# An RWKV-6 attention feeding a GELU MLP: third token blocks paired from the first tile on

## Chip, cores and metric

The kernel runs on one core of one Trainium2 chip. The metric is the device time of one execution in microseconds (us). Before the change it is 604.43 us (median of three runs, 604.32 to 604.50). The profile is one execution with a span of 601.6 us from the first to the last instruction; the granted TensorE clock was full throughout.

Short names in what follows: PE is TensorE, DVE is VectorE, ACT is ScalarE, SP is SyncE.

## What is computed

A recurrent attention over 768 time steps (batch 4, 8 heads, head size 48), and then a two-layer MLP with exact GELU on its output, 3072 tokens of width 384, hidden width 2048:

```python
for t in range(S):                                   # attention, per batch and head
    cur = einsum('bhd,bhe->bhde', u[None] * k[t], v[t])
    y[t] = einsum('bhd,bhde->bhe', r[t], state + cur)
    state = w[t][..., None] * state + einsum('bhd,bhe->bhde', k[t], v[t])

x = y.transpose(0, 2, 1, 3).reshape(3072, 384)       # bridge
h = x @ w_in                                         # 3072x384 @ 384x2048
g = 0.5 * h * (1 + erf(h / sqrt(2)))
out = g @ w_out                                      # 3072x2048 @ 2048x384
```

All values are float32.

## The kernel before

The tokens are worked in eight tiles of 384 (x = 0 to 7). `attention(x)` makes one tile's attention output `xT`; `mlp(x)` turns it into 384 rows of the result. Both are generators: each `yield` ends a step, and a driver decides which step of the one is issued between which steps of the other. While the MLP of tile x-1 runs, the attention of tile x is woven into it. [...]

In the second product of the MLP, a tile has three blocks of 128 tokens. Blocks 0 and 1 are multiplied with `w_out` as a 2x2 block matrix product with seven instead of eight block products (Winograd's form, with sums made beforehand by DVE). The third block of a tile cannot be paired within its tile, so it is paired with the third block of the next tile, which gives one more product of that kind. The tile that comes first of a pair (`waits`) computes two of the products and keeps its GELU output in `alone`; the second (`ends`) computes the other five. Before, the pairs are tiles (1,2), (3,4), (5,6). The first tile (x = 0) multiplies all its three blocks in the plain way, the last (x = 7) its third block.

```python
NX = 8; T = 384; NF = 16; HF = 8; HM = 192; BANK = 512
ps = ...  # PSUM, tag "mm": two banks, shared by h_ps, o_ps and the y_ps of one part
pd = ...  # PSUM, tag "d": three pairs of banks, for the attention

def mlp(x):
    halves = x > 0
    waits, ends = x % 2 == 1 and x < NX - 1, x % 2 == 0 and x > 0
    final = x == NX - 1
    if final:
        h_halves()        # first product of the last tile, itself with seven of eight products
    for group in (() if final else (0, 2, 1, 3) if halves else range(4)):     # 16 steps
        for f in range(group * FG, (group + 1) * FG):
            # h_ps = w_in block f times xT: three matmuls of 384 columns
            t = T - 128 if waits else T
            nc.scalar.activation(out=gs[group][:, f % FG, 0:t], in_=h_ps[:, 0:t], func=AF.Gelu)
            if waits:
                nc.scalar.activation(out=alone[:, f], in_=h_ps[:, t:], func=AF.Gelu)
            yield
    if final:             # the third block of the last tile, alone: 16 matmuls of 384 columns
        ... nc.tensor.matmul(o_ps, lhsT=block(2, f // HF, f % HF), rhs=w_out_sb[:, f, :], ...)
        nc.scalar.copy(out=o_sb, in_=o_ps); store(x * T + 256, o_sb)
        yield
    if halves:            # seven products of 8 matmuls of 192 columns, a step each (steps 16 to 22)
        ...
    if waits:             # two products, steps 23 and 24
        _, o2, o1 = psum(), psum(), psum()
        product(o2, of_alone(0), of_w(0, 0), True); nc.scalar.copy(out=p1_alone, in_=o2)
        yield
        product(o1, of_alone(1), of_w(1, 0), True)
        nc.vector.tensor_add(o_sb[:, 0:HM], o1, p1_alone); store(...)
        yield
    elif ends:            # five products, steps 23 to 27
        ...
    elif not final:       # x = 0: blocks 0 and 1 together (steps 16 to 31), then block 2 (32 to 47)
        for blocks in (0, 1), (2,):
            o_ps = [ps.tile([128, BANK], F32, name="o_ps", tag="mm", bufs=2)[:, 0:DM] for _ in blocks]
            for f in range(NF):
                for i, o in zip(blocks, o_ps):
                    nc.tensor.matmul(o, lhsT=block(i, f // HF, f % HF), rhs=w_out_sb[:, f, :], ...)
                if f < NF - 1:
                    yield
            for i, o in zip(blocks, o_ps):
                o_sb = wk.tile([128, DM], F32, name="o_sb", bufs=2)
                nc.vector.tensor_copy(out=o_sb, in_=o); store(x * T + i * 128, o_sb)
            yield
```

The last stretch of `attention(x)` issues the products with the states (PE, into `y_ps`) and takes the result out of PSUM. From tile 1 on it does the latter on ACT, with DMAs that carry a part of it to other partitions:

```python
        nc.tensor.matmul(ys[b][0][c % 2]..., lhsT=src[...], rhs=rc[...], ...)    # 48 of them
        ...
        copy = nc.vector.tensor_copy if x == 0 else nc.scalar.copy
        copy(out=xT[s, pair, :]..., in_=y[s])               # six copies of 48x384 (x > 0)
        ...
        nc.scalar.copy(out=ysb..., in_=y)                   # one of 128x384, before the six
        (nc.scalar if z * NJ + j > (2 if x == 0 else 3) else nc.sync).dma_start(out=xT[...], in_=ysb[...])
```

Tiles 0 and 1 do the lower triangle of the attention in six levels (h = 1 to 32), each with products on PE, an update of r and k by decays on DVE (one instruction), and a copy into `a_sb`. Later tiles do two levels of four. In tile 0, which works its heads in two units, the k of the last level is then transposed on PE, and r is used much later, for the products with the states.

The driver (cut), and the sums of blocks of `w_out`, which DVE makes once, in eight instructions a step each:

```python
def w_sums():        # sums[0] to sums[3]: eight tensor_sub of 128x768, one to a step
    ...
    shares = chain(weight_in(gate=True), second, weight_in(gate=True), weight_in(gate=True))
    ...
    convert()
    for unit in (0, 0, 1, 0, 0, 1, 1, 0, 1):
        next(units[unit])
    keep_warm(6, True)
    convert()

    for x in range(1, NX):
        place = [1, 3, 5, 7, 9, 11, 13, 15, 18, 20, 26, 32] if x == 1 else [1, 6, 8, 13, 15, 16, 18, 18, 20, 21]
        place_next = [38, 47] if x == 1 else [21, 24] if x % 2 == 0 else [25, 27]
        loads = load(x + 1, nc.scalar if x > 1 else nc.sync)
        times = range(20, 30) if x == 1 else (2, 3, 4, 5, 16, 17, 18, 19, 20, 21)
        more = iter(())
        for step, _ in enumerate(mlp(x - 1)):
            if x == 1 and step == 2 * NF - 2:
                make_quarter_masks(); more = w_sums()
            next(more, None)
            if x == 1 and step in (0, 2, 4, ..., 24):
                convert()                        # a piece of the weights, four DVE and two ACT instructions
            if step in times:
                next(loads, None)                # a piece of tile x+1
            while place and place[0] <= step:
                place.pop(0); next(slots, None)  # a step of attention(x)
            while place_next and place_next[0] <= step:
                place_next.pop(0); next(following, None)     # the first two steps of attention(x+1)
```

Of the kernel before, what the change touches and what calls it, by code (L numbers as in the profile page):

```python
# [23 lines left out]
T = 384  # L24
# [20 lines left out]
def kernel(  # L45
# [79 lines left out]
    def load_second(dma):  # L125

        loaded[1] = [None, None]
        for i in range(SHARES):
            s = slice(i * 3 * ALL // SHARES, (i + 1) * 3 * ALL // SHARES)
            nc.vector.memset(bufs[1][:, s.start:s.start + 1], 0.0)  # L130
            dma.dma_start(out=bufs[1][:, s], in_=rkw[1, :, s])
            yield
        load_v(1, dma)
        yield
# [185 lines left out]
    def attention(x, unit):  # L320
# [102 lines left out]
        def halves():  # L423

            for h in LEVELS:
# [14 lines left out]
                t2 = tot[h].rearrange("p (n two) -> p n two", two=2)[:, :, 0:1].to_broadcast(r2.shape)  # L440
                rk = bass.AP(tensor=r2.tensor, offset=r2.offset, ap=[r2.ap[0], [n_u - h, 2]] + list(r2.ap[1:]))
                tt = bass.AP(tensor=t2.tensor, offset=t2.offset, ap=[t2.ap[0], [1, 2]] + list(t2.ap[1:]))
                nc.vector.tensor_mul(rk, rk, tt)  # L443
# [118 lines left out]

        yield from halves() if x < 2 else quarters()
# [89 lines left out]
        if x == 0:  # L653

            inside()
            yield
            chain_states()
            yield
            fences()
        else:  # L660
            chain_states()
            yield
            inside()
            fences()
            yield
# [68 lines left out]
    def h_sums():  # L734
# [14 lines left out]
        for i in range(4):  # L749
            for k in range(2):  # L750
                if i == 0:
                    nc.vector.tensor_add(s(1, k), w(1, 0, k), w(1, 1, k))
                elif i == 1:
                    nc.vector.tensor_sub(s(2, k), s(1, k), w(0, 0, k))
                elif i == 2:
                    nc.vector.tensor_sub(s(3, k), w(0, 0, k), w(1, 0, k))
                else:
                    nc.vector.tensor_sub(s(4, k), w(0, 1, k), s(2, k))
            if i < 3:
                yield  # L760
# [9 lines left out]
    def mlp(x):  # L770
# [5 lines left out]
        waits, ends = x % 2 == 1 and x < NX - 1, x % 2 == 0 and x > 0  # L776
# [24 lines left out]
        def h_halves():  # L801
# [9 lines left out]
            for f in range(HF):  # L811
# [11 lines left out]
                def s(i):  # L823
                    return in_s[i - 1][:, f // FI, f % FI * 128:(f % FI + 1) * 128]
# [12 lines left out]
                for z in late:  # L837
                    gelu(*z)
                multiply(b_6, (s(2), in_t[1]))
# [7 lines left out]
                multiply(b_4, (w(1, 1), in_t[3]), (w(1, 2), last[0]))  # L847
                nc.vector.tensor_add(c21, b_4, u3)
                gelu(1, 0, c21)
                multiply(b_0, (w(1, 2), last[1]))  # L850
                nc.vector.tensor_add(c22, b_0, u5)
                gelu(1, 1, c22)
# [60 lines left out]
        if final:  # L913
            o_ps = ps.tile([128, BANK], F32, name="o_ps", tag="mm", bufs=2)[:, 0:DM]
            order = [f for f in range(NF) if f % HF < HF - 1] + [HF - 1, NF - 1]
            for n, f in enumerate(order):
                nc.tensor.matmul(o_ps, lhsT=block(2, f // HF, f % HF), rhs=w_out_sb[:, f, :], start=(n == 0), stop=(n == NF - 1))  # L917
            o_sb = wk.tile([128, DM], F32, name="o_sb", bufs=2)
            nc.scalar.copy(out=o_sb, in_=o_ps)
            store(x * T + 256, o_sb)  # L920
            yield


        if halves:
            row0 = x * T
# [41 lines left out]


        if waits:
            _, o2, o1 = psum(), psum(), psum()  # L970
# [34 lines left out]
        elif not final:  # L1005

            for blocks in (0, 1), (2,):
                o_ps = [ps.tile([128, BANK], F32, name="o_ps", tag="mm", bufs=2)[:, 0:DM] for _ in blocks]
                for f in range(NF):
                    for i, o in zip(blocks, o_ps):  # L1010
                        nc.tensor.matmul(o, lhsT=block(i, f // HF, f % HF), rhs=w_out_sb[:, f, :],  # L1011
                                         start=(f == 0), stop=(f == NF - 1))
                    if f < NF - 1:
                        yield
                for i, o in zip(blocks, o_ps):
                    o_sb = wk.tile([128, DM], F32, name="o_sb", bufs=2)
                    nc.vector.tensor_copy(out=o_sb, in_=o)  # L1017
                    store(x * T + i * 128, o_sb)
                yield
# [5 lines left out]
    shares = chain(weight_in(gate=True), second, weight_in(gate=True), weight_in(gate=True))  # L1025
# [19 lines left out]
    convert()  # L1045

    for unit in (0, 0, 1, 0, 0, 1, 1, 0, 1):
        next(units[unit])
# [6 lines left out]

    for x in range(1, NX):

        place = [1, 3, 5, 7, 9, 11, 13, 15, 18, 20, 26, 32] if x == 1 else [1, 6, 8, 13, 15, 16, 18, 18, 20, 21]
        place_next = [38, 47] if x == 1 else [21, 24] if x % 2 == 0 else [25, 27]
        loads = load(x + 1, nc.scalar if x > 1 else nc.sync)  # L1060

        times = range(20, 30) if x == 1 else (2, 3, 4, 5, 16, 17, 18, 19, 20, 21)
        following = attention(x + 1, 0) if x + 1 < NX else iter(())
        more = iter(())
        for step, _ in enumerate(mlp(x - 1)):
# [4 lines left out]
            next(more, None)  # L1070
# [10 lines left out]
            if x == NX - 1:  # L1081

                if step == 18:
                    more_h = h_sums()
                for _ in range({18: 1, 22: 2, 25: 1}.get(step, 0)):
                    next(more_h)
# [65 lines left out]
```

## Time and profile before

| What | Before |
|---|---|
| time, median of three | 604.43 us |
| span of the profile | 601.6 us |
| PE busy, matmuls | 586.7 us (98%) |
| PE weight loads busy | 455.5 us (76%) |
| DVE busy | 468.4 us (78%) |
| ACT busy | 178.9 us (30%) |
| moved by DMA | 46.72 MB, 78 GB/s in the mean |

The busy row of an engine is its share of the whole span; whether an engine bounds a stage is read from the stage. One matmul of float32 shows as two instructions in the profile, so the counts of matmuls there are twice those of the code. The stages that matter, in us from the start: tile 0's attention up to 42.9, `mlp(0)` from 42.9 to 125.3, then `mlp(1)` to `mlp(6)` with 65 or 73 us each, and `mlp(7)` from 541.1 to the end.

### The profile page before, as it was taken

The page shows a single profiled execution, that of the slowest core. Times are in us where ns is not written, and L with a number is a line of the kernel's source. Part 1 is how long each engine was busy: PE and PEld are TensorE (multiplying, and loading weights), DVE is VectorE, ACT ScalarE, POOL GpSimd, SP SyncE. Part 2 cuts the span into 40 slices and gives each one's busy share as a digit, 9 for nine tenths or more (in the row PEclk, how much of TensorE's full clock was granted, in tenths as well). Part 3 has the DMA queues.
Part 4 walks back from the last instruction along what each step waited for, and adds up shares of the span by engine and source line. Part 5 has one row for each costly group of instructions (what it writes and reads, how often), then busy time and mean ns, then how long its engine had stood idle before and what let it go on. Part 6 is the DMA issues. An engine that isn't in the chain of part 4 may idle for free.

```text
span 601.6 us, 16117 instructions
## 1 busy us (share of the span) xinstructions
PE 586.7 (98%) x6993; PEld 455.5 (76%) x7008; DVE 468.4 (78%) x896; ACT 178.9 (30%) x414; POOL 8.4 (1%) x24
## 2 busy tenths in 40 slices
PE   8779999999999999999999999999999999999997
PEld 4556566656798669986699568995689668999977
DVE  8979999998866978488884987679786888665701
ACT  2446476213223322213222232113222133024400
POOL 3100000000000000000000000000000000000000
PEclk9999999999999999999999999999999999999999
DMA  5775348111141305203052304213052002010000
GB/s 201 253 239 194 110 162 297 38 46 60 25 123 45 92 2 111 73 21 93 1 112 73 99 1 83 87 36 92 3 111 73 8 1 40 16 38 8 1 14 26
DMA packets 50566, 46.72 MB, mean 78 GB/s; under 512 B 31680, under 2 KB 35904, under 8 KB 50496
## 3 DMA queue, kind: packets, MB, share of 16 engines
q1 hardware_dynamic: 33152, 29.31, 15.8%
q10 hardware_dynamic: 17344, 16.39, 10.1%
q8 instruction: 55, 0.90, 0.6%
q14 instruction: 15, 0.12, 0.1%
HBM read 36.24 MB, written 4.72 MB: 68 GB/s over the span
## 4 chain that ended last, share of the span: by engine, by line
PE 71%; DMA 1%; issue 0%; DVE 0%; ACTq 0%
PE o_ps L888 30%; PE h_ps L874 26%; PE b L828 5%; PE d L521 4%; PE o_ps L917 2%; PE kv_ps L598 2%; PE y_ps L639 2%; PE y_ps L677 1%; DMA rkw<-kx 1%; PE d L514 1%; DVE o_sb L960 0%; ACTq L468 0%
## 5 line engine op out<-in xcount | busy, mean ns | idle before, releaser
L874 PE MATMUL h_ps<-xT,w_in_sb 128*128 128x384 f32 x672 | 223.0, 489 | 0.0
L874 PEld LDWEIGHTS h_ps<-xT,w_in_sb 128*128 128x128 f32 x672 | 125.9, 190 | 84.6 <-ACT xT L684 0.4
L877 ACT ACTIVATE g<-h_ps 128x384 f32<-128x384 f32 (+1 forms) x112 | 49.4, 443 | 168.3 <-PE h_ps L874 168.3
L888 PE MATMUL o_ps<-t,s 128*128 128x192 f32 x480 | 81.9, 329 | 0.0
L888 PEld LDWEIGHTS o_ps<-t,s 128*128 128x128 f32 x480 | 77.8, 190 | 0.7
L552 DVE COPY_PREDICATED a_sb<-quarter,d 128x384 f32<-128x384 uint8 (+2 forms) x108 | 45.1, 438 | 2.5
L888 PE MATMUL o_ps<-w_out_sb,g 128*128 128x192 f32 x224 | 38.7, 326 | 0.0
L888 PEld LDWEIGHTS o_ps<-w_out_sb,g 128*128 128x128 f32 x224 | 37.0, 190 | 1.9
L613 DVE SCALAR_TENSOR_TENSOR st<-st,tot_sb,kv_ps 128x48 f32<-128x48 f32 x160 | 29.0, 259 | 4.1 <-PE kv_ps L598 4.1
L1011 PE MATMUL o_ps<-w_out_sb,g 128*128 128x384 f32 x96 | 32.2, 491 | 0.0
L888 PE MATMUL o_ps<-w_out_sb,s 128*128 128x192 f32 x160 | 28.3, 330 | 0.0
L888 PE MATMUL o_ps<-t,g 128*128 128x192 f32 x160 | 27.6, 326 | 0.0
L408 PEld LDWEIGHTS d<-rkw 64*64 64x64 f32 x1152 | 18.6, 134 | 11.8 <-DVE rkw L443 7.8
L1011 PEld LDWEIGHTS o_ps<-w_out_sb,g 128*128 128x128 f32 x96 | 17.8, 190 | 12.3 <-DVE o_sb L1017 0.6
L345 DVE TRANSPOSE_TENSOR_REDUCE rkw<-kx 128x48 f32<-128x1536 f32 (+3 forms) x24 | 26.8, 1155 | 0.2
L521 PEld LDWEIGHTS d<-kx,rkw 64*64 64x64 f32 x1152 | 24.3, 133 | 3.4 <-DVE a_sb L559 1.6
L521 PE MATMUL d<-kx,rkw 64*64 64x96 f32 x1152 | 26.5, 245 | 0.0
L888 PEld LDWEIGHTS o_ps<-t,g 128*128 128x128 f32 x160 | 26.3, 190 | 0.0
L888 PEld LDWEIGHTS o_ps<-w_out_sb,s 128*128 128x128 f32 x160 | 25.9, 190 | 0.4
L408 PE MATMUL d<-rkw 64*64 64x64 f32 (+1 forms) x1152 | 20.9, 221 | 4.6 <-DVE rkw L443 2.9
L534 DVE TENSOR_TENSOR rkw<-rkw,tot_sb 128x768 f32<-128x768 f32 x12 | 11.5, 958 | 17.4 <-PE d L521 17.4
L381 DVE TENSOR_TENSOR rkw<-rkw 128x384 f32<-128x384 f32 (+2 forms) x24 | 23.6, 1004 | 0.4
(148 smaller groups left out, 741.8 us busy)
## 6 DMA issues: line engine op xcount, KB each, us to landing
rkw<-in_rkw_dram ACTq DMA_DIRECT2D x45, 256.0 KB, 2.8
raw<-in_w_out_dram SPq DMA_DIRECT2D x8, 768.0 KB, 4.4
out_dram<-o_sb SPq DMA_DIRECT2D x21, 192.0 KB, 1.9
raw<-in_w_in_dram SPq DMA_DIRECT2D x5, 768.0 KB, 6.0
v_in<-in_v_dram ACTq DMA_DIRECT2D x5, 584.0 KB, 3.7
raw<-in_w_in_dram SPq DMA_DIRECT2D x9, 256.0 KB, 3.8
rkw<-in_rkw_dram SPq DMA_DIRECT2D x8, 288.0 KB, 3.4
rkw<-in_rkw_dram SPq DMA_DIRECT2D x9, 256.0 KB, 7.5
```

What stands on the lines that cost most here:

```text
L345: nc.vector.tensor_reduce(out=fine_sb[:, e, 0:n].rearrange("p a n -> p (a n)"), in_=kx[:, o:o + n * n_m].rearrange("p (m j) -> p m j", j=3 ...
L381: nc.vector.tensor_mul(z, z, by)
L408: nc.tensor.matmul(d[half[p], g, n * width:(n + 1) * width], lhsT=kc[half[g], b, i, p], rhs=right(half[g], b, i, p), start=True, stop=True)
L521: nc.tensor.matmul(d[half[p], g, i * 3 * C // 2:(i + 1) * 3 * C // 2], lhsT=kc[half[g], (n + i) // NI, (n + i) % NI, p], rhs=rx[half[g], 2 ...
L552: nc.vector.copy_predicated(out=an[:, :, :, :, (a + 1) * h:], mask=mask.to_broadcast(data.shape), data=data)
L598: nc.tensor.matmul(kv_ps[half[g], p, i * D:(i + 1) * D], lhsT=k_t(b, i, p, g), rhs=vs(b, i, g)[half[p], 0:D], start=True, stop=True)
L613: nc.vector.scalar_tensor_tensor(out=stq[:, q, c], in0=stq[:, q, c - 1] if c else b4[:, q, NC - 1], scalar=totq[:, q, c:c + 1], in1=kvs[q ...
L828: nc.tensor.matmul(o, lhsT=lhsT, rhs=rhs, start=start and i == 0, stop=(i == len(factors) - 1), skip_group_check=True)
L874: nc.tensor.matmul(h_ps, lhsT=w_in_sb[:, f // FI, j, f % FI * 128:(f % FI + 1) * 128], rhs=xT[:, j, :], start=(j == 0), stop=(j == NJ - 1))
L877: nc.scalar.activation(out=gs[group][:, f % FG, 0:t], in_=h_ps[:, 0:t], func=AF.Gelu)
L888: nc.tensor.matmul(o, lhsT=lhs(j), rhs=rhs(j), start=start and j == 0, stop=(j == HF - 1), skip_group_check=True)
L1011: nc.tensor.matmul(o, lhsT=block(i, f // HF, f % HF), rhs=w_out_sb[:, f, :], start=(f == 0), stop=(f == NF - 1))
```

## The change

The pairs of third blocks become (0,1), (2,3), (4,5), (6,7), so that no third block is multiplied in the plain way any more. With this the roles swap: even tiles wait, odd ones end. `mlp(0)` then has 34 steps instead of 48, and what was woven into them is placed anew; the two PSUM results of `mlp(0)` are copied by ACT instead of DVE, and four of the eight sums of `w_out` blocks move to `mlp(1)`. The loads of k and w of a coming tile are issued a step later. In tile 0, the update of the last level is split, k's part first and r's part after the next products, and the conversion of a weight piece and the copies of one unit move off the way of the other unit. In the last tile's first product, two products that need no sums come first. Cut to its core:

```diff
@@ load_second
-        load_v(1, dma)
-        yield
@@ attention, levels of tiles 0 and 1
+                def update(z, r2=r2, t2=t2, k2=k2, tk=tk):
+                    nc.vector.tensor_mul(*((k2, k2, tk) if z is k else (r2, r2, t2)))
+                if x == 0 and m == 1:
+                    update(k)
+                    last_r.append(lambda: update(r))
+                else:
                     nc.vector.tensor_mul(rk, rk, tt)
@@ attention, tile 0, after the products inside the chunks
             inside()
             yield
+            for z in last_r:
+                z()
+            yield
             chain_states()
-            yield
             fences()
+            yield
@@ h_sums
-            if i < 3:
-                yield
+            yield
@@ mlp
-        waits, ends = x % 2 == 1 and x < NX - 1, x % 2 == 0 and x > 0
+        waits, ends = x % 2 == 0, x % 2 == 1
@@ h_halves, for each f
+                multiply(b_0, (w(1, 2), last[1]))
+                multiply(b_4, (w(1, 2), last[0]))
                 multiply(b_6, (s(2), in_t[1]))
 ...
-                multiply(b_4, (w(1, 1), in_t[3]), (w(1, 2), last[0]))
+                nc.vector.tensor_add(c22, b_0, u5)
+                gelu(1, 1, c22)
+                multiply(b_4, (w(1, 1), in_t[3]), start=False)
                 nc.vector.tensor_add(c21, b_4, u3)
                 gelu(1, 0, c21)
-                multiply(b_0, (w(1, 2), last[1]))
-                nc.vector.tensor_add(c22, b_0, u5)
-                gelu(1, 1, c22)
@@ mlp, second product
-        if final:
 ...                                  (the plain third block of the last tile goes)
-        elif not final:
 ...                                  (the plain blocks (0, 1) and (2,) of tile 0 go)
+        else:
+            o_ps = [ps.tile([128, BANK], F32, name="o_ps", tag="mm", bufs=2)[:, 0:DM] for _ in range(2)]
+            for f in range(NF):
+                for i, o in enumerate(o_ps):
+                    nc.tensor.matmul(o, lhsT=block(i, f // HF, f % HF), rhs=w_out_sb[:, f, :], start=(f == 0), stop=(f == NF - 1))
+                if f < NF - 1:
+                    yield
+            for i, o in enumerate(o_ps):
+                o_sb = wk.tile([128, DM], F32, name="o_sb", bufs=2)
+                nc.scalar.copy(out=o_sb, in_=o)
+                store(row0 + i * 128, o_sb)
+            yield
         if waits:
-            _, o2, o1 = psum(), psum(), psum()
+            if halves:
+                psum()
+            o2, o1 = psum(), psum()
@@ driver
-    shares = chain(weight_in(gate=True), second, weight_in(gate=True), weight_in(gate=True))
+    shares = chain(weight_in(gate=True), islice(second, 5), weight_in(gate=True), second, weight_in(gate=True))
-    convert()
-    for unit in (0, 0, 1, 0, 0, 1, 1, 0, 1):
+    load_v(1, nc.sync)
+    piece = conversion()
+    next(piece)
+    for unit in (0, 0, 0, 1, 0, 0, 1, 1, 1):
+        next(units[unit])
+    for _ in piece:
+        pass
+    for unit in (0, 1):
         next(units[unit])
+    more = iter(())
-        place = [1, 3, 5, 7, 9, 11, 13, 15, 18, 20, 26, 32] if x == 1 else ...
-        place_next = [38, 47] if x == 1 else [21, 24] if x % 2 == 0 else [25, 27]
+        place = [1, 3, 5, 7, 9, 11, 13, 15, 18, 20, 26, 30] if x == 1 else ...
+        place_next = [31, 33] if x == 1 else [25, 27] if x % 2 == 0 else [21, 24]
-        times = range(20, 30) if x == 1 else (2, 3, 4, 5, 16, 17, 18, 19, 20, 21)
+        times = range(18, 28) if x == 1 else (2, 3, 4, 5, 17, 18, 19, 20, 21, 22)
-        more = iter(())
-            next(more, None)
+            if x == 1 or step > 8:
+                next(more, None)
-                for _ in range({18: 1, 22: 2, 25: 1}.get(step, 0)):
+                for _ in range({18: 1, 20: 1, 22: 2, 23: 1}.get(step, 0)):
```

More of the change, by code (lines that the diff above doesn't have):

```diff
@@ L1 @@
 import struct
-from itertools import chain
+from itertools import chain, islice
 from contextlib import ExitStack
@@ L440, in halves @@
                 t2 = tot[h].rearrange("p (n two) -> p n two", two=2)[:, :, 0:1].to_broadcast(r2.shape)
+                k2 = k.rearrange("p (n two j) -> p n two j", two=2, j=h)[:, :, 0, :]
+                tk = tot[h].rearrange("p (n two) -> p n two", two=2)[:, :, 1:2].to_broadcast(k2.shape)
                 rk = bass.AP(tensor=r2.tensor, offset=r2.offset, ap=[r2.ap[0], [n_u - h, 2]] + list(r2.ap[1:]))
                 tt = bass.AP(tensor=t2.tensor, offset=t2.offset, ap=[t2.ap[0], [1, 2]] + list(t2.ap[1:]))
-                nc.vector.tensor_mul(rk, rk, tt)
+                def update(z, r2=r2, t2=t2, k2=k2, tk=tk):
[4 more added lines that the diff above has]
+                else:
+                    nc.vector.tensor_mul(rk, rk, tt)
                 ah = at.rearrange("p g n (m two j) -> p g n m two j", two=2, j=h)[:, :, :, :, 1, :]
@@ L561, in quarters @@
                 yield
+        last_r = []
         yield from halves() if x < 2 else quarters()
@@ L656, in attention @@
             yield
+            for z in last_r:
+                z()
+            yield
             chain_states()
+            fences()
             yield
-            fences()
         else:
@@ L910, in two_rows @@
             return [wk.tile([128, DM], F32, name="o_sb", bufs=2) for _ in range(2)]
-        if final:
[L914 to L920, printed above, removed]
-            yield
+        row0 = x * T
         if halves:
-            row0 = x * T
             o_sb = two_rows()
@@ L1004, in mlp @@
             yield
-        elif not final:
[L1007 to L1019, printed above, removed]
     units = [attention(0, unit) for unit in range(units_of(0))]
     second = load_second(nc.sync)
-    shares = chain(weight_in(gate=True), second, weight_in(gate=True), weight_in(gate=True))
+    shares = chain(weight_in(gate=True), islice(second, 5), weight_in(gate=True), second, weight_in(gate=True))
     for unit in units:
@@ L1052 @@
     next(slots)
+    more = iter(())
     for x in range(1, NX):
-        place = [1, 3, 5, 7, 9, 11, 13, 15, 18, 20, 26, 32] if x == 1 else [1, 6, 8, 13, 15, 16, 18, 18, 20, 21]
-        place_next = [38, 47] if x == 1 else [21, 24] if x % 2 == 0 else [25, 27]
+        place = [1, 3, 5, 7, 9, 11, 13, 15, 18, 20, 26, 30] if x == 1 else [1, 6, 8, 13, 15, 16, 18, 18, 20, 21]
+        place_next = [31, 33] if x == 1 else [25, 27] if x % 2 == 0 else [21, 24]
         loads = load(x + 1, nc.scalar if x > 1 else nc.sync)
-        times = range(20, 30) if x == 1 else (2, 3, 4, 5, 16, 17, 18, 19, 20, 21)
+        times = range(18, 28) if x == 1 else (2, 3, 4, 5, 17, 18, 19, 20, 21, 22)
         following = attention(x + 1, 0) if x + 1 < NX else iter(())
-        more = iter(())
         for step, _ in enumerate(mlp(x - 1)):
```

## The prediction, as written before the result was known

> **What bounds the kernel now.** I read the chain of waits first, then the stages one by one, then the timelines of single engines around the places that the change touches. The chain, merged in order of time, is PE almost without a break from tile 2's stage on; columns are start, length, what:
>
> ```profile
> 170.16 0.14 issue
> 170.29 1.73 PE kv_ps L598 x92
> 172.02 5.40 PE o_ps L888 x32
> ...
> 541.06 28.60 PE b L828 x176
> 569.66 10.32 PE o_ps L917 x32
> 579.98 18.21 PE o_ps L888 x112
> ```
>
> So the time is the sum of PE's work plus the few places where PE stands still. Two prices come from here: the plain third block of the last tile is 32 instructions in 10.32 us, 322 ns each (384 columns); a product in halves is 16 instructions, and 112 of them take 18.21 us, 163 ns each (192 columns); over a stretch with weaves the page gives 165. Half the columns cost half the time, so a seven-of-eight form is a true saving on PE.
>
> The stages show who is near its limit (columns: window, length, then busy us and count of PE, PE weight loads, DVE, ACT, POOL, clock, DMA):
>
> ```profile
> 42.90:125.30 82.40, 81.11 (x1165) 51.73 (x1165) 80.05 (x124) 41.86 (x63) 0.00 (x0) 1.00 0.46 156
> 125.30:191.10 65.80, 65.66 (x722) 51.15 (x721) 51.69 (x95) 18.23 (x54) 0.00 (x0) 1.00 0.26 67
> 191.10:264.18 73.08, 73.08 (x785) 58.67 (x785) 57.31 (x105) 17.59 (x39) 0.00 (x0) 1.00 0.23 59
> 402.92:467.98 65.06, 65.06 (x722) 50.66 (x721) 51.51 (x95) 18.24 (x54) 0.00 (x0) 1.00 0.26 69
> ```
>
> In `mlp(0)`, the first row, PE and DVE are both full (81.1 and 80.1 of 82.4 us); afterwards DVE has over 13 us to spare in each stage shown. The reader should also see 65.80 against 65.06: two of the three waiting stages lose about 0.7 us.
>
> ACT's timeline at the end of `mlp(0)` shows what happens when tile 1's attention output leaves PSUM. It comes after the products with the states, which PE starts at 113.97:
>
> ```profile
> 115.67 0.48 ACT L703 COPY ysb<-y_ps 128x384 f32<-128x384 f32 x1 [12.96 <-PE y_ps L677]
> 116.18 1.42 ACTq L707 DMA_DIRECT2D xT<-ysb  x2
> 117.64 2.89 ACT L700 COPY xT<-y_ps 48x384 f32<-48x384 f32 x6 [1.49 <-issue]
> ```
>
> ACT is bound for 4.9 us (115.67 to 120.53) and does nothing else in that time.
>
> [...] an instruction with a wait holds what follows (L930 sits behind the DMA issues of L468 for 3.9 us). [...] Here the MLP's rotation has two banks. [...]
>
> **The change, part by part.**
>
> A. Third blocks. Gone: 64 instructions of 384 columns, 2 x 10.32 = 20.6 us. New: a fourth pair, seven products of 16 instructions, 112 x 0.1645 = 18.4 us. PE **-2.2 us**. By stage: `mlp(0)` -10.3 + 2 x 2.63 = -5.1; the odd ones +7.9, the even ones -7.9; `mlp(7)` -10.3 + 13.2 = +2.9. In the later stages DVE's pair work moves with PE's, so they stay PE's: even `mlp(1)`, with 51.7 us of DVE before, some 5.5 us of pair sums and 3.7 us of `w_out` sums, stays at 61 of 74 us.
>
> B. The copies on ACT in `mlp(0)`. The last attention step is placed at step 30, and the output copies are issued in step 31, so in ACT's queue they stand **behind** L703, two DMA issues and six L700. After the products with the states PE has one step left, 4 instructions, 1.29 us. Then the first `alone` product needs the bank of `o_ps`: both banks of the tag are held by the two results. It comes free after 4.9 us of attention copies and 0.5 us for a 128x384 copy (L877's size; L703 shows 0.48), with about 0.15 us for signals: 5.6 us. PE stands still for 5.6 - 1.3 = **+4.3 us**. DVE would have been free: before, L1017 did this at once. This is the term on which my number rests.
>
> C. DVE relief in `mlp(0)`: four sums less (4 x 0.95) and three L1017 less (3 x 0.56), 5.5 us, about what PE loses. So DVE does not become the bound. PE's small waits in L1011 for L1017 and L316 (0.6 + 0.4 us before) mostly go: **-0.6**.
>
> D. Start. PE before `mlp(0)` follows a chain through DVE:
>
> ```profile
> 29.16 0.96 DVE L443 TENSOR_TENSOR rkw<-rkw,tot_sb 128x768 f32<-128x768 f32 x1 [0.44 <-PE d L408]
> ...
> 30.26 0.84 PE L572 MATMUL kt_ps<-ident,rkw 128*128 128x128 f32 x6 [0.85 <-DVE raw L174]
> ...
> 38.71 1.12 DVE L700 COPY xT<-y_ps 48x384 f32<-48x384 f32 x2
> 39.85 0.22 DVE L649 COPY fence<-y_ps 128x1 f32<-128x1 f32 x2
> 40.13 1.24 PEld L677 LDWEIGHTS y_ps<-rkw,st 64*64 64x64 f32 x40 [1.81 <-DVE fence L649]
> ```
>
> With k alone the update is 384 columns, 0.56 us instead of 0.96 (L309 and L499 show 0.55 for elementwise work on 128x768 in place or 128x384): transposes 0.4 us earlier. The 1.12 us of L700 and the last 0.96 us of a conversion leave the way of the fence; r's 0.56 us for the other unit comes into it. Part is kept by a break of 1.5 us in PE's issue at 34.6 to 36.1, which no instruction explains and which may stay. Between 0.45 and 1.4 us: **-1.0**.
>
> E. Four sums in `mlp(1)`, at steps 9 to 12. They stand on DVE before the second level's updates. DVE has only 1.49 us of slack there (L534 waits that long for PE at 158.11), so 4 x 0.91 - 1.49 = 2.2 us reach the transposes of k and its DMAs, and through ACT's queue the copy L930, which at an ending stage is done 1.6 us before the third product needs it. With the DMA's landing I count **+0.8**.
>
> F. Loads of k and w a step later: the copies L582 no longer stand behind the first load's issue (0.79 + 0.52 us at 166.65 and 167.60), and PE's wait before L598 in waiting stages shrinks. Of the 1.34 us lost before ((65.80 - 65.06) + (65.66 - 65.06)) half: **-0.7**. In a waiting stage, though, the last piece of w at step 22 now stands behind L703 and L700 on ACT and lands close to the moment when the first L377 needs it: **+0.3**.
>
> G. The last store has half the columns; the first product of the last tile has the same work, and the products that follow need GELUs that are 2.6 us old: **-0.1**.
>
> Sum: -2.2 + 4.3 - 0.6 - 1.0 + 0.8 - 0.7 + 0.3 - 0.1 = **+0.8 us**, so 604.4 + 0.8 = **605.2 us**.
>
> **Rivals.** (1) The bank is not waited for: ACT takes the output copies before the attention's, or the attention step ends early enough. Then B is nought and the time is about 601 us. For it: the whole point of moving the copies is to free DVE, and the last step was put two steps earlier. Against it: the order of issue, and that ACT takes 4.9 us where PE has 1.3 us of work. (2) DVE becomes the bound of `mlp(0)`: at 77 us with 74.5 us of DVE it has no room for waits of its own; a slip of the conversions would add 1 to 3 us on top: 606 to 608. Against it: the profile's first part of that stage is unchanged. (3) The sums in `mlp(1)` push the k DMAs out by more than E says, and PE waits at L598 for the whole 2.2 us: 606.6. (4) The start brings more, if the break in PE's issue goes with the new order of loads: 603.5.
>
> **Range and chances.** B is worth 4.3 us and I give rival 1 some 15 in 100; the other terms are each uncertain by 0.5 to 1 us and together by about 1.5. The range is 601.8 to 607.2 us. 2% is 12 us, which no sum of these terms reaches: within 2% 0.98, faster 0.01, slower 0.01.
>
> **What would show it.** A: L917 gone, L888 with 1232 instead of 1120 instructions, odd stages near 73 us and even ones near 65. B: at the end of `mlp(0)` PE idle some 4 us before the first L888, with ACT as the releaser, the output copy right behind six L700. C: no wait of PE for L1017. D: the first L874 at 42 us instead of 42.9. E: L534 of tile 2 with no wait for PE, L930 late. F: short stages all near 65.0 us. The prediction is wrong if PE is idle nowhere near the end of `mlp(0)`, or if a stage from `mlp(2)` on has new waits of over 1 us.

## The result, and the profile after

| What | Before | After |
|---|---|---|
| time, median of four runs each | 604.38 us | 611.32 us |
| ratio after / before, 95% interval | | 1.0119 (1.0081 to 1.0158) |
| span of the profiled execution | 601.6 us | 607.9 us |

The kernel became 1.2% slower, about 7 us (the interval is clear of 1). The prediction was 605.2 us, and the time lies above its range (601.8 to 607.2).

First the stages of after, which answer to the four rows shown of before (the same columns: window, length, busy us and count of PE, PE weight loads, DVE, ACT, POOL, clock, DMA share, then two columns that aren't used here): `mlp(0)`, `mlp(1)`, `mlp(2)` and `mlp(5)`:

```profile
41.60:127.11 85.51, 79.26 (x1164) 53.99 (x1165) 74.62 (x117) 43.44 (x82) 0.00 (x0) 0.96 0.48 162
127.11:202.51 75.40, 73.75 (x771) 58.92 (x770) 61.88 (x112) 17.46 (x39) 0.00 (x0) 1.00 0.22 57
202.51:267.79 65.28, 65.28 (x737) 50.87 (x737) 51.15 (x93) 18.15 (x54) 0.00 (x0) 1.00 0.26 69
405.93:478.79 72.86, 72.86 (x770) 58.45 (x769) 57.64 (x107) 17.48 (x39) 0.00 (x0) 1.00 0.22 59
```

Two things stand out. `mlp(0)` has less PE work than before (79.3 us against 81.1) and is still 3.1 us longer, and it is the one row whose clock is not 1.00. And `mlp(1)` is 2.5 us longer than `mlp(5)`, which does the same kind of work. Subtracting the stages of the two traces gives the whole difference of 6.3 us in the span (`mlp(7)` is counted from its first product, which starts at 540.90 in before and at 543.91 in after):

| Stretch | Before | After | Difference |
|---|---|---|---|
| up to the first product of h | 42.9 | 41.6 | -1.3 |
| `mlp(0)` | 82.4 | 85.5 | +3.1 |
| `mlp(1)` | 65.8 | 75.4 | +9.6 |
| `mlp(2)` to `mlp(6)` | 349.8 | 341.4 | -8.4 |
| `mlp(7)`, to the end of PE | 57.3 | 60.9 | +3.6 |
| tail | 3.4 | 3.1 | -0.3 |

If only the pairing of the third blocks had changed, `mlp(0)` would have come to -5.1, `mlp(1)` to +7.9, the five in the middle to -7.9 and `mlp(7)` to +2.9 (the prediction's part A). So `mlp(0)` is 8.2 us too long, and that is the first place to look. Its end in windows of 5 us (the same columns):

```profile
110.00:115.00 5.00, 4.87 (x106) 2.84 (x104) 4.97 (x17) 0.48 (x1) 0.00 (x0) 1.00 0.01 3
115.00:120.00 5.00, 1.13 (x4) 1.14 (x5) 3.75 (x4) 3.70 (x8) 0.00 (x0) 0.81 0.18 50
120.00:125.00 5.00, 5.00 (x18) 5.00 (x17) 0.00 (x0) 0.32 (x1) 0.00 (x0) 0.51 0.16 58
125.00:130.00 5.00, 5.00 (x23) 3.82 (x23) 2.60 (x4) 0.49 (x1) 0.00 (x0) 1.00 0.06 20
```

In the second row PE does almost nothing; in the third it is busy all the time, but at half its clock (0.51). The timeline of ACT in after tells why PE stood still (start, length, what, and the idle time before with its releaser):

```profile
113.45 0.48 ACT L715 COPY ysb<-y_ps 128x384 f32<-128x384 f32 x1 [10.76 <-PE y_ps L689]
113.96 1.42 ACTq L719 DMA_DIRECT2D xT<-ysb  x2
115.42 2.90 ACT L712 COPY xT<-y_ps 48x384 f32<-48x384 f32 x6 [1.49 <-issue]
118.33 0.86 ACT L979 COPY o_sb<-o_ps 128x384 f32<-128x384 f32 x2
```

And the timeline of PE in after for the same moment:

```profile
113.31 1.56 PE L974 MATMUL o_ps<-w_out_sb,g 128*128 128x384 f32 x4
...
118.87 8.41 PE L900 MATMUL o_ps<-w_out_sb,rkw 128*128 128x192 f32 x32 [4.00 <-ACT o_sb L979]
```

The wait is the predicted one: the output copy L979 stands right behind six copies L712, and PE waits 4.00 us for it. The L974 products that the copy reads ended at 114.87 us, and ACT took it up at 118.33, with the six copies that were issued ahead of it done first; PE began 0.05 us after the first of the two copies had ended (the prediction's 0.15 us for signals was its author's estimate). The new thing is the 8.41 us behind it: two products of 16 instructions, which at the prediction's price of 164.5 ns would take 5.26 us.

In the last tile, the chain of waits of after answers to the last three lines shown of before; the 176 instructions that had been one block of 28.60 us are broken in two:

```profile
544.07 5.30 PE b L839 x32
...
550.82 22.81 PE b L839 x136
573.63 31.21 PE o_ps L900 x192
```

Here L917 is gone, and the second product is 192 instructions in 31.21 us, where before it was 32 + 112 in 28.53 us.

### The profile page after: what moved, and what is told of

Read it like the earlier page. It is cut to its first block, busy times and chain, and to the rows that moved or that the text cites. A ratio compares the mean times of both kernels' runs of the same rounds, so it can differ in the third digit from the quotient of the medians.

```text
span 607.9 us, 16255 instructions
## 1 busy us (share of the span) xinstructions
PE 588.5 (97%) x7041; PEld 464.3 (76%) x7056; DVE 473.1 (78%) x909; ACT 179.8 (30%) x434; POOL 8.4 (1%) x24
## 4 chain that ended last, share of the span: by engine, by line
PE 84%; DVE 11%; issue 2%; ACT 1%; DMA 1%; SPq 0%; ACTq 0%; DVEq 0%
PE o_ps L900 33%; PE h_ps L886 29%; PE b L839 5%; PE d L529 4%; PE o_ps L974 3%; PE d L406 2%; PE kv_ps L607 2%; PE y_ps L689 2%; PE y_ps L648 2%; DVE rkw L451 1%; PE warm L194 1%; DVE a_sb L461 1%; DVE rkw L379 1%; PE d L522 1%; DVE kx L350 1%
## 5 line engine op out<-in xcount | busy, mean ns | idle before, releaser
L889 ACT ACTIVATE g<-h_ps 128x256 f32<-128x256 f32 (+1 forms) x112 | 47.6, 428 | 169.8 <-PE h_ps L886 169.8
L900 PE MATMUL o_ps<-t,s 128*128 128x192 f32 x528 | 89.8, 328 | 0.0
L900 PEld LDWEIGHTS o_ps<-t,s 128*128 128x128 f32 x528 | 85.6, 190 | 0.7
L900 PE MATMUL o_ps<-w_out_sb,g 128*128 128x192 f32 x224 | 38.8, 326 | 0.3 <-ACT p L931 0.3
L900 PEld LDWEIGHTS o_ps<-w_out_sb,g 128*128 128x128 f32 x224 | 36.9, 190 | 2.2 <-ACT p L931 0.6
L900 PE MATMUL o_ps<-w_out_sb,s 128*128 128x192 f32 x176 | 31.0, 330 | 0.0
L900 PE MATMUL o_ps<-t,g 128*128 128x192 f32 x176 | 30.4, 326 | 0.0
L900 PEld LDWEIGHTS o_ps<-t,g 128*128 128x128 f32 x176 | 28.9, 190 | 0.0
L900 PEld LDWEIGHTS o_ps<-w_out_sb,s 128*128 128x128 f32 x176 | 28.6, 190 | 0.4
L406 PEld LDWEIGHTS d<-rkw 64*64 64x64 f32 x1152 | 18.8, 134 | 13.2 <-DVE rkw L451 7.3
L900 PE MATMUL o_ps<-w_out_sb,rkw 128*128 128x192 f32 x128 | 24.5, 356 | 4.0 <-ACT o_sb L979 4.0
L900 PEld LDWEIGHTS o_ps<-w_out_sb,rkw 128*128 128x128 f32 x128 | 23.8, 212 | 4.6 <-ACT o_sb L979 4.6
L529 PEld LDWEIGHTS d<-kx,rkw 64*64 64x64 f32 x1152 | 24.3, 133 | 3.8 <-issue 1.6
L406 PE MATMUL d<-rkw 64*64 64x64 f32 (+1 forms) x1152 | 21.3, 221 | 5.8 <-DVE rkw L451 2.9
L529 PE MATMUL d<-kx,rkw 64*64 64x96 f32 x1152 | 26.5, 245 | 0.3 <-DVE kx L508 0.3
L502 ACT COPY kx<-rkw 128x384 f32<-128x384 f32 x36 | 16.1, 508 | 26.4 <-PE d L529 15.4
```

Source lines behind the costliest of these rows:

```text
L406: nc.tensor.matmul(d[half[p], g, n * width:(n + 1) * width], lhsT=kc[half[g], b, i, p], rhs=right(half[g], b, i, p), start=True, stop=True)
L502: nc.scalar.copy(out=z, in_=r4[:, :, :, f, :])
L529: nc.tensor.matmul(d[half[p], g, i * 3 * C // 2:(i + 1) * 3 * C // 2], lhsT=kc[half[g], (n + i) // NI, (n + i) % NI, p], rhs=rx[half[g], 2 ...
L900: nc.tensor.matmul(o, lhsT=lhs(j), rhs=rhs(j), start=start and j == 0, stop=(j == HF - 1), skip_group_check=True)
```

## The experiments

Each ratio below is to the kernel before, with its 95% interval, from runs on the same chip. Spans and lengths are from one profiled execution each.

**The gap and the clock.** Three kernels change only the end of `mlp(0)`. `copies_dve` gives the two output copies back to DVE:

```diff
-                nc.scalar.copy(out=o_sb, in_=o)
+                nc.vector.tensor_copy(out=o_sb, in_=o)
```

> The changed kernel with its two output copies of mlp(0) back on DVE. Theory (ACT's queue holds the banks for 4.0 us, and this gap then halves PE's clock for the two products behind it, 8.41 us instead of 5.26): both go, 4.0 + 3.1 = 7 us less than the changed kernel, some 604 us, and the granted clock is 1.000. Rival 1 (the clock drop has another cause than the gap): only 4 us less, some 607 us, and those two products still take 8.4 us. Rival 2 (DVE is so full in mlp(0) that its copies come late as well): PE waits for DVE there for over 1 us, less than 3 us gained.

Measured: 1.0021 (1.0004 to 1.0038), 1.0% under after. PE's timeline of this kernel:

```profile
115.65 1.56 PE L974 MATMUL o_ps<-w_out_sb,g 128*128 128x384 f32 x4
117.21 5.47 PE L900 MATMUL o_ps<-w_out_sb,rkw 128*128 128x192 f32 x32
...
142.86 2.21 PE L529 MATMUL d<-kx,rkw 64*64 64x96 f32 x96 [1.52 <-DVE kx L508]
```

The gap is gone and the same 32 instructions take 5.47 us. `mlp(0)` is 78.6 us instead of 85.5: 4.0 from the gap and 8.41 - 5.47 = 2.9 from the clock make 6.9. The cost moves in part to DVE: its L979 copies wait 1.91 us for PE in DVE's queue, the attention of tile 2 starts later, L529 waits 1.52 us, and `mlp(1)` is 76.7 us.

`warm_gap` keeps the wait and fills it with 18 products of zeros, whose result nobody reads:

```diff
         if waits:
+            if not halves:
+                keep_warm(18, True)
```

> The changed kernel with 18 matmuls of zeros (128x512, bf16) into a spare bank, put between the last plain product of mlp(0) and its two products of the third block; they fill some 3.8 of the 4.0 us in which PE waits for ACT, and take no wait away. Theory: the wait stays (the two products start 4 us after the plain ones end), but they run at full clock, 5.3 us instead of 8.4: 3.1 us less than the changed kernel, some 608 us. Rival 1 (the clock does not depend on the gap): no gain, 611 us.

Measured: 1.0063 (1.0044 to 1.0082), 0.56% or 3.4 us under after. PE's timeline:

```profile
118.47 4.05 PE L194 MATMUL warm<-zeros 128*128 128x512 bf16 x18
122.67 5.47 PE L900 MATMUL o_ps<-w_out_sb,rkw 128*128 128x192 f32 x32 [0.16 <-ACT o_sb L979]
```

L979 still releases the products no earlier; only PE's idle time is gone, and with it the slow clock. This separates the two: idle time costs 4.0 us, and the slow clock that follows costs 2.9 us by the trace of after and 3.4 by the times, where the two intervals leave 2.6 us to either side. What is left in `warm_gap` is the wait: it lies 0.63% or 3.8 us above `place31` (below), which has no gap. (The profiled execution itself had a span of 608.0 us, as long as that of after, because its `mlp(0)` started 2.1 us later and the clock was 0.79 in the mean from 48 to 56 us. Single spans scatter in this way, which is why verdicts rest on ratios.)

`warm_half` fills only half of the gap, with 9 products instead of 18:

```diff
-                keep_warm(18, True)
+                keep_warm(9, True)
```

> The changed kernel with only 9 matmuls of zeros (some 2 us) at the start of the gap in which PE waits for ACT; 2 us of idle time remain. If only a gap of several us lowers the clock, the two products run in 5.4 us at full clock, as with 18. If any gap does, they take 7 to 8 us.

A single run, 607.62 us. PE's timeline, whose group has eight of the nine:

```profile
115.16 2.11 PE L194 MATMUL warm<-zeros 128*128 128x512 bf16 x8
...
119.32 5.47 PE L900 MATMUL o_ps<-w_out_sb,rkw 128*128 128x192 f32 x32 [2.05 <-ACT o_sb L979]
```

An idle time of 2.05 us left the clock at 1.00; one of 4.00 in after halved it to 0.50. What a gap between these two does was not measured.

`place31` lets the attention's last step be issued a step later, behind the output copies; nothing else is changed against after:

```diff
-        place = [1, 3, 5, 7, 9, 11, 13, 15, 18, 20, 26, 30] if x == 1 else ...
+        place = [1, 3, 5, 7, 9, 11, 13, 15, 18, 20, 26, 31] if x == 1 else ...
```

> The changed kernel with the last step of tile 1's attention one step later (31 instead of 30), so that the output copies, still on ACT, stand ahead of the attention's copies in ACT's queue, and the products with the states lie between. Theory (the order in ACT's queue, not ACT's speed, makes the gap): the gap of 4.0 us and the slow clock go; as xT is then made later, up to 0.5 us may be waited before mlp(1): some 604 to 605 us. Rival 2 (ACT is simply too slow for the copies): less than half of the 7 us gained, 608 us or more.

Measured: 1.0000 (0.9981 to 1.0019). ACT's timeline:

```profile
114.53 0.48 ACT L979 COPY o_sb<-o_ps 128x384 f32<-128x384 f32 x1 [9.79 <-PE o_ps L974]
115.18 0.48 ACT L979 COPY o_sb<-o_ps 128x384 f32<-128x384 f32 x1 [0.17 <-PE o_ps L974]
116.77 0.48 ACT L715 COPY ysb<-y_ps 128x384 f32<-128x384 f32 x1 [1.11 <-PE y_ps L689]
```

The same copies on the same engine, the other way round: the gap and the slow clock are gone, and `mlp(0)` is 78.6 us. So the order in ACT's queue made the gap, not ACT's speed. One number in a list was worth 7 us. (PE's products with the states move with the step, behind the last plain products.)

**The order of the first product in the last tile.** `h_order` is after with the products of `h_halves` in the order of before:

```diff
-                multiply(b_0, (w(1, 2), last[1]))
-                multiply(b_4, (w(1, 2), last[0]))
                 multiply(b_6, (s(2), in_t[1]))
 ...
-                nc.vector.tensor_add(c22, b_0, u5)
-                gelu(1, 1, c22)
-                multiply(b_4, (w(1, 1), in_t[3]), start=False)
+                multiply(b_4, (w(1, 1), in_t[3]), (w(1, 2), last[0]))
 ...
+                multiply(b_0, (w(1, 2), last[1]))
+                nc.vector.tensor_add(c22, b_0, u5)
+                gelu(1, 1, c22)
```

> The changed kernel with the order of products in the last tile's first product as before the change. Theory (the new order makes PE wait for the sums on DVE, 29.7 us instead of 28.6 in the traces): 1.1 us less than the changed kernel, the stage back at 28.6 us. Rival (the stage is longer for the products of sums that come late at its start): no gain, or a loss of 0.5 us, as the sums of xT are then needed sooner.

Measured: 1.0077 (1.0050 to 1.0105), which is 0.42% under after but overlaps its interval; the trace decides. Its chain of waits has the 176 instructions whole again:

```profile
543.47 28.60 PE b L839 x176
```

In after the same chain has them from 544.07 to 573.63 (the lines shown above): 29.56 us, 1.0 more. The costliest groups of after, by shape, name the product (columns: instructions, busy us and mean ns of one, idle us just before):

```profile
L839 PE MATMUL b<-xT,w_in_sb 128*128 128x192 f32 x96 | 18.4, 326 | 0.0
L839 PE MATMUL b<-xT,rkw 128*128 128x192 f32 x16 | 4.5, 365 | 0.2 <-DVE rkw L857 0.2
```

Only `b<-xT,rkw`, the second part of `b_5`, is longer than the rest: 365 ns instead of 326, and 0.2 us of idle time, with L857 (`u5`) as the releaser. Little of the loss shows as idle time: in each of the eight rounds the first of the two instructions takes 0.40 to 0.43 us instead of 0.33 and holds up the next by 0.07 to 0.10, and in the second round it also starts 0.32 us late. That makes the 1.0 us. The second part writes into the bank that `u5` reads. Between the two parts of `b_5` PE had ten instructions before (`b_1` x4, `b_4` x4, `b_0` x2, at 163 ns each 1.63 us) and has six now (0.98 us), because the `b_0` and `b_4` products were moved ahead. That is the time which DVE has for its chain `u2`, `u3`, `u5`.

In `h_order` the gap at the end of `mlp(0)` was 4.01 us again, but the products behind it took 7.13 us instead of 8.41: how long the slow clock lasts differs from one execution to another (the last section says by what steps).

**The sums of `w_out` in `mlp(1)`.** `late_sums` is `place31` with less on DVE in front of tile 2's attention: `mlp(0)` makes its four sums a step earlier (two in the first step), and of the four in `mlp(1)` two stay at steps 9 and 10 and two go to steps 19 and 20; the order of the sums becomes 0, 1, 3, 2, so that those needed last are made last:

```diff
-        for i, (x, y) in enumerate((...)):
+        for i in (0, 1, 3, 2):
 ...
-            if x == 1 or step > 8:
+            if x == 1 and step < 2 * NF + 1 or step in (9, 10, 19, 20):
+                next(more, None)
+            if x == 1 and step == 2 * NF - 2:
                 next(more, None)
```

> The kernel place31 with the sums of w_out placed anew: the fourth before the third block's products of mlp(0), the two that are needed first at steps 9 and 10 of mlp(1), the last two (needed at step 21) at steps 19 and 20, where DVE has gaps. Theory (the four sums at steps 9 to 12 push the transposes of k, and through them ACT's copy and the k DMAs, so that mlp(1) lasts 75.0 us and not 72.9 like the other ending stages): mlp(1) at about 73.5 us, 1.5 us less than place31. Rival (mlp(1) is long as attention(2) starts late on DVE, and the loads of k in its DMAs are slow whatever the sums do): mlp(1) stays at 74.5 us or more.

Measured: 0.9974 (0.9959 to 0.9989), 0.26% under `place31`, though the intervals overlap; here too the traces decide. PE in `place31`:

```profile
168.72 1.69 PE L607 MATMUL kv_ps<-v_in,rkw 64*64 64x48 f32 x92 [1.13 <-DMA rkw<-kx]
```

and in `late_sums`:

```profile
168.02 1.61 PE L607 MATMUL kv_ps<-v_in,rkw 64*64 64x48 f32 x96
```

The wait for the DMA of k is gone, and `mlp(1)` falls from 75.0 to 73.1 us, close to the other stages of its kind (72.9).

**Both together.** `best` is `late_sums` with the order of `h_order`; no line is new.

> The kernel late_sums with the order of products in the last tile's first product as before the change. Theory: 1.0 us less than late_sums (that stage 28.6 us instead of 29.6), 2.5 us less than place31, and so under the kernel before by 2 to 3 us: ratio 0.995 to 0.997. Rival: the terms do not add, and it stays within 0.2% of the kernel before.

Measured: 0.9943 (0.9924 to 0.9962), 601.36 us, span 599.4. It beats both kernels, by 0.6% and 1.8%. `place31`, which has the shorter products too, was only level with before, because E and G (below) ate what they bring; without both, the gain is there. Its first three stages, in the columns used above:

```profile
43.09:121.57 78.48, 76.21 (x1165) 51.00 (x1165) 75.48 (x118) 43.56 (x82) 0.00 (x0) 1.00 0.53 176
121.57:194.94 73.37, 73.37 (x769) 58.96 (x770) 60.83 (x111) 17.56 (x39) 0.00 (x0) 1.00 0.22 59
194.94:260.23 65.29, 65.29 (x738) 50.88 (x737) 51.13 (x93) 18.14 (x54) 0.00 (x0) 1.00 0.26 69
```

In `mlp(1)` and `mlp(2)` PE is now busy from end to end.

**The loads of k and w.** `best_times` is `best` with the steps of the loads as before:

```diff
-        times = range(18, 28) if x == 1 else (2, 3, 4, 5, 17, 18, 19, 20, 21, 22)
+        times = range(18, 28) if x == 1 else (2, 3, 4, 5, 16, 17, 18, 19, 20, 21)
```

> The kernel best with the loads of k and w at their steps of before (16 to 21 instead of 17 to 22). Theory (a load's issue ahead of the copies L582 made PE wait 0.6 us before the products of k and v in some of the waiting stages): mlp(2) and mlp(4) at 65.7 us instead of 65.3, some 0.8 us more in all. Rival (the waits there come from the k DMAs, and the last load of w, now behind ACT's copies, costs as much): within 0.2 us of best.

Measured: 0.9985 (0.9968 to 1.0001), 0.42% or 2.5 us over `best`. Its `mlp(2)`:

```profile
197.91:264.00 66.09, 65.69 (x738) 51.18 (x737) 51.18 (x93) 18.23 (x54) 0.00 (x0) 1.00 0.26 68
```

66.09 us against 65.29 in `best`, and `mlp(4)` 66.0 against 65.3. ACT's timeline of `best_times` shows a likely reason: the issue of a load stands ahead of the copies L591, which are the way of k to PE:

```profile
238.95 0.60 ACTq L146 DMA_DIRECT2D rkw<-in_rkw_dram  x1
239.59 0.51 ACT L591 COPY rkw<-kx 32x384 f32<-32x384 f32 x1 [0.35 <-issue]
```

But the order alone does not cost: `start_only` (next) has the loads at these steps too and the issue ahead of the copies (167.69 and 168.49 us in its trace), and all three of its waiting stages take 65.05 us, with no wait of PE. There ACT comes to these copies earlier: 3.3 us before PE's products with k and v, against 2.7 us in `best_times`.

**The start.** `start_only` is the kernel before with nothing but the new start (k's part of the last update first, r's part later, a conversion put off, v of tile 1 loaded after the weights):

```diff
-    shares = chain(weight_in(gate=True), second, weight_in(gate=True), weight_in(gate=True))
+    shares = chain(weight_in(gate=True), islice(second, 5), weight_in(gate=True), second, weight_in(gate=True))
 ...
-    convert()
-    for unit in (0, 0, 1, 0, 0, 1, 1, 0, 1):
+    load_v(1, nc.sync)
+    piece = conversion()
+    next(piece)
+    for unit in (0, 0, 0, 1, 0, 0, 1, 1, 1):
 ...                                       (and the three parts in the attention)
```

> The kernel before with only the start of the change: the update of the last level split into k's and r's part, the conversion of a weight piece and one unit's copies moved off the other unit's way, the weights' and tile 1's loads in the new order; pairs, copies and sums as before. Theory: from tile 0's last level to the first matmul of mlp(0) the traces showed 16.1 us before and 14.5 us after; so 1.6 us less than the kernel before, some 0.3%. Rival (the shorter way is given back in mlp(0), where DVE has to do the same conversions): less than 0.5 us.

Measured: 1.0005 (0.9985 to 1.0025). The new start alone is worth nothing that can be measured. PE's timeline of `start_only` shows a loss in tile 1's first products:

```profile
47.60 1.58 PE L406 MATMUL d<-rkw 64*64 64x32 f32 x91
50.12 0.31 PE L406 MATMUL d<-rkw 64*64 64x32 f32 x5 [0.94 <-issue]
```

Before, these 96 ran without a stop. "issue" means that no instruction which the profile shows was waited for. The stop lies in the same place in after. From 46 to 50 us the DMA share is 1.00 to 1.04 in after and in `start_only`, and 0.65 to 0.76 before: with the conversion put off, the loads of the next weights are put off too, and five pieces are then loaded in a row, where before loads one of them early.

`best_load` and `start_load` make that load early again, in `best` and in `start_only`:

```diff
     next(piece)
+    for _ in weight_in():
+        pass
```

> The kernel best with the first weight piece that has no gate (256 KB x 3, into a buffer that is free already) loaded right after the first half of the first conversion, before the units' last steps, instead of after it with the next four. Theory (PE's issue stops for 0.9 us after the 91st of the 96 first products of tile 1's attention since the pieces loaded together keep the DMA engines full from 44 to 52 us, where before they were at 0.65 to 0.76; every such stop lies 254 matmuls after the one before[...]): that stop shrinks to 0.3 us or less, mlp(0) is 0.6 to 0.9 us shorter. Rival (the stop belongs to the new order of instructions, not to the DMAs): it stays at 0.9 us, no gain.

> The kernel start_only with the same early load of one weight piece. Theory: the stop of 0.94 us in the first products of tile 1's attention goes, mlp(0) lasts 82.5 us as in the kernel before instead of 83.7, and the gain of the start is kept: 0.2 to 0.3% under the kernel before. Rival: no change against start_only, 0 to 0.1%.

Measured: 0.9949 (0.9929 to 0.9969) and 0.9995 (0.9975 to 1.0014), no gain in either. The stop in L406 is gone, but another has come earlier. PE in `start_load`:

```profile
41.65 0.69 PE L689 MATMUL y_ps<-rkw,st 64*64 64x64 f32 x17 [1.83 <-issue]
```

and in `best_load`:

```profile
42.94 1.12 PE L689 MATMUL y_ps<-rkw,st 64*64 64x64 f32 x17 [2.10 <-issue]
```

So a full DMA goes with the stops, but moving a load only moved the stop: in `best_load` `mlp(0)` is 1.4 us shorter than in `best`, and starts 3.1 us later. The theory of the simultaneous loads is half supported at best; the last section has what the traces say of the stops.

## Why the prediction was wrong, point by point

**B, the gap (predicted +4.3): right in its mechanism and size, and short of the truth by the clock.** PE stood still for 4.00 us, with ACT as the releaser and L979 behind six L712, as written. The step that failed is in A and B together: the two products behind the gap were priced at 2.63 us each, as if the clock stayed. They took 8.41 us; without a gap they take 5.47. This is 2.9 us, the largest of the errors, and `warm_gap` shows that it comes from the idle time and not from the wait.

**E, the four sums (predicted +0.8): mechanism right, size too small.** `mlp(1)` has 75.4 us against 72.9 in `mlp(3)` and `mlp(5)`, so about 2.5 us is lost there in after; `late_sums`, which moves only the sums, brings 1.9 of `place31`'s 2.1 back. The failing term is "4 x 0.91 - 1.49 = 2.2 us reach the transposes", of which I let only 0.8 reach PE. It comes close to rival 3, the whole 2.2 us at the products with kv, but over several waits rather than one: after's timeline of PE shows 1.03 us at L607 for the DMA of k, 0.28 us at L900 for a copy on ACT and 0.34 us at L529 for DVE.

**G, the last tile (predicted -0.1): wrong.** The diff for `h_halves` was read as a change that moves no cost. It costs 1.0 us: 29.56 against 28.60 us, and `h_order` and `best` have 28.60 again. I counted the work of PE, which is the same, and not the time that PE leaves DVE between two writes to one bank.

**D, the start (predicted -1.0): the chain it worked on did become shorter, and the time did not.** From the start of the last L408 products ahead of the transposes (L406 in after) to the first product of h, before needs 42.89 - 28.16 = 14.7 us and after 41.62 - 28.48 = 13.1 us. The part from the update to the transposes is 0.4 us shorter, as worked out. The other kernels with this start have 13.1 to 13.6 us there, except `best_load` and `start_load`; the 13.6 belong to `best` and `start_only`, which have a stop of 1.51 us on the way as before's trace has, so at an equal stop 1.1 us is gained. But they reach these products later, at 28.42 to 30.82 us; before's one trace reaches them at 28.16. On the way there most of them show stops of PE's issue of 0.3 to 1.4 us, before's trace none, though the stops don't account for all of the delay; then comes the stop of 0.94 us at the start of `mlp(0)`. `start_only` gives the sum: nothing. The step that failed is the allowance for a break in PE's issue: the prediction expected the one of 1.5 us at most to stay, and not others around it.

**A, the pairing (predicted -2.2): right.** L917 is gone, L900 has 1232 instructions, the odd stages from `mlp(3)` on are 72.9 us and the even ones 65.3. In `mlp(7)`, 192 instructions take 31.21 us against 28.53 for the old mixture: 2.7 us, predicted 2.9.

**F, the loads (predicted -0.7 and +0.3): a gain in `best`, not shown in after.** `mlp(2)` to `mlp(6)` gained 8.4 us, 0.5 beyond the pairing's 7.9. But in `start_only`, which has the loads at the old steps, these stages are 0.6 us shorter than before as well, so the 0.5 can't be put down to the shift; and with the shift, `place31` still waits 0.47 us at L607 in `mlp(4)`. Taking the shift back costs `best` 2.5 us (the two intervals together leave about 1.5 us to either side); the two stages named above account for 1.5 us of it. No late piece of w is seen in the waiting stages of after, which are all at 65.3.

**C, DVE relief (predicted -0.6): misread.** The 0.6 + 0.4 us of waits in L1011 were those of the weight loads, which overlap the products (51.73 us of loads and 81.11 us of products in the stage's 82.40 us); PE itself stood idle in before's `mlp(0)` only at L408 (0.65 and 0.63 us, for DVE's updates), and these two waits are still there in after (0.65 and 0.64 at L406). So there was nothing to gain. `mlp(0)` without gap and slow clock is 78.6 us, 1.3 us over the 77.3 which A alone would leave; 0.94 us of it is the stop of the issue.

The terms side by side, in us, for the profiled executions of before and after:

| Term | Predicted | Found |
|---|---|---|
| A, pairing | -2.2 | -2.4 |
| B, idle time of PE | +4.3 | +4.0 |
| slow clock behind it | 0 | +2.9 |
| C and what else is in `mlp(0)` | -0.6 | +1.2 |
| D, up to the first product of h | -1.0 | -1.3 |
| E, `mlp(1)` beyond the pairing | +0.8 | +1.7 |
| F, `mlp(2)` to `mlp(6)` beyond the pairing | -0.4 | -0.5 |
| G, order of the last tile's products, tail | -0.1 | +1.0 - 0.3 |
| sum | +0.8 | +6.3 |

The range failed for the same reason as the number: it allowed for B being absent, and for nothing that B might set off.

## What to carry to other kernels

Price an idle gap of PE with the work behind it: a gap of 4.0 us cost 6.9 us in one trace and 5.7 in another, one of 2.05 us only itself, and with useless products in the gap (9 or 18 here) the products behind it took 5.47 us instead of 8.41. When a copy that frees a PSUM bank moves to an engine with time to spare, look at what stands in front of it in that engine's queue at that moment; the order of issue was worth 7 us, the choice of the engine next to nothing (`copies_dve` and `place31` differ by 0.2%, with overlapping intervals). And when products are put in another order, count what PE has to do between two writes to one bank (here 1.63 us before and 0.98 us after) and hold it against the chain that must read the bank in between; here the shorter stretch cost 1.0 us.

## What the runs showed of the hardware that I had not expected

**Half the clock followed gaps of 4.00 us and not one of 2.05, and the slow time came in steps of 3.41 us.** 4.00 us of idle time (after) and 4.01 (`h_order`) were followed by a clock of 0.50; behind 2.05 us (`warm_half`) it stayed at 1.00. The traces have the moments at which the clock changes. In after it falls at 118.05 and rises at 124.88 us:

```profile
114.64:118.05 3.41, 0.23 (x1) 0.00 (x0) 3.38 (x5) 2.58 (x6) 0.00 (x0) 1.00 0.18 43
118.05:121.47 3.42, 2.60 (x8) 2.60 (x9) 0.74 (x1) 1.12 (x3) 0.00 (x0) 0.50 0.32 115
121.47:124.88 3.41, 3.41 (x13) 3.41 (x12) 0.00 (x0) 0.32 (x1) 0.00 (x0) 0.50 0.00 0
```

In `h_order` it falls at 118.81 and is back at 122.22:

```profile
115.40:118.81 3.41, 0.00 (x0) 0.00 (x1) 3.29 (x3) 3.33 (x8) 0.00 (x0) 1.00 0.14 34
118.81:122.22 3.41, 3.41 (x11) 3.41 (x12) 0.00 (x0) 0.33 (x1) 0.00 (x0) 0.50 0.32 115
```

The slow time is 6.83 us in the one and 3.41 in the other, which is why the products behind the same gap lost 2.9 and 1.7 us. Five other traces (`warm_gap`, `late_sums`, `best_times`, `best_load`, `start_load`) have one slow stretch each, between 40 and 56 us, and it too is 3.4 us long by the clock of the windows there. In after the first stretch at full clock lasts 112.64 us and the one behind the slow time 484.69 us, which are 33 and 142 times 3.413 us; in before the only one lasts 597.33 us, 175 times that. So in these two traces every change of the clock lies a whole number of steps of 3.41 us from the one ahead of it. The step before the fall at the gap had 0.23 us of PE's work in after and none in `h_order`; in `warm_half` the 4.12 us ahead of the two products (115.20 to 119.32 us) had 2.01 us of it, and no fall.

**The clock also fell where no such gap was.** Two windows of the same stretch, in `late_sums`:

```profile
48.00:52.00 4.00, 3.06 (x68) 2.01 (x61) 3.86 (x8) 1.16 (x3) 0.00 (x0) 0.79 1.02 363
```

and in `best`:

```profile
48.00:52.00 4.00, 3.06 (x59) 2.12 (x52) 3.83 (x9) 1.04 (x3) 0.00 (x0) 1.00 1.01 362
```

Both have the same stop of 0.94 us and the same 3.06 us of PE, and one runs at 0.79: it is at half the clock from 50.29 to 53.70 us. In the 3.41 us before that fall PE had 2.48 us of work, and `best` has stretches of the same length with 2.47 us (48.01 to 51.42) and 1.91 us (34.35 to 37.77) and no fall, so in these traces PE's busy time alone does not decide. What does stays open.

**PE's stops of issue lay 254 weight loads apart in after, each 1.2 to 1.5 us behind a packet of one DMA queue.** In the first 52 us of after PE has three stops of over 0.15 us that no instruction explains: 0.26 us up to 26.23, 0.96 us up to 35.51 and 0.94 us up to 48.18. They lie 254 weight loads apart (they come after 39 of the 48 products of one level, 31 of the kv products, 91 of tile 1's first products); with a matmul to each weight load and PE's few other instructions that is 511 and 512 instructions. In `best` the stop at L406 lies 254 weight loads behind the one at L607 too, and in `best_load`, with the early load, the stop at L689 lies 128 behind it. One DMA queue, which the page of after calls "instruction" (columns: packets, MB, share), moved packets of 16,384 bytes:

```profile
q8 instruction: 56, 0.92, 0.6%
```

Three of these packets landed at 25.01, 34.03 and 46.73 us, 1.2 to 1.5 us before the ends of the three stops; in before PE has one such stop in that time, 1.51 us up to 36.14, and a packet landed 1.6 us before its end, at 34.53. But six of the nine packets that landed in the first 52 us of after, and eight of the nine in before, were followed by no such stop. The DMA share around the three stops of after is 0.62 (25 to 27 us), 0.89 (34 to 36.5) and 1.01 (46 to 50), and stops take up to 2.10 us (`best_load`). A stop of 0.21 us at L598 of before, at 309.07 us, does not follow this: it ends 12.8 us after a packet. No run changes these packets alone, so what stops PE's issue was not shown.
